# A chunked attention and MLP kernel whose order of issue is planned: fetches of TensorE's instructions enter the plan, two inversions change engine, the filler changes type

## The chip, the cores and the metric

One core of a Trainium2 chip runs the kernel. The metric is device time in microseconds of one execution, the median of three runs. TensorE is called PE below, VectorE DVE, ScalarE ACT, GpSimd POOL; SP is the engine whose queue issues every DMA of this kernel.

## The reference

```
for t in range(768):                                  # state: [4, 8, 40, 40], from zeros
    y[t]  = einsum('bhd,bhde->bhe', r[t], state)
    Sa    = einsum('bhde,bhe->bhd', state, a[t])
    state = state * w[t] - einsum('bhd,bhe->bhde', Sa, b[t]) + einsum('bhd,bhe->bhde', v[t], k[t])
x  = y as [4, 768, 320]
xn = (x - mean) / sqrt(var + 1e-6) * g_ln             # over the 320
out = x + relu(xn @ w_ch1) @ w_ch2                    # w_ch1 320x1280, w_ch2 1280x320
```

All data are fp32: 32 heads (4 x 8) of 40, 768 steps.

## The kernel before

The 768 steps are cut into 24 chunks of 32. Inside a chunk the recurrence is a triangular system for each head. `prep` scales the inputs of a chunk by running products of w (`L436`, `L445` scans on DVE; `aT` at L454 and `bk` at L464 on DVE or POOL) and PE multiplies them (`tri`, L492); DVE puts the result into `gk`, and a DMA writes it to DRAM as `d_g`. The chunks of a **slab** are inverted together: the slabs are chunks 0-1, 2-3, 4-7, 8-11, 12-15, 16-19 and 20-23, numbered 0 to 6 here and in the code. A DMA (L526) brings a slab's matrices into `yi`, one per partition; `invert` runs elimination steps on them, two instructions each; a DMA (L558) writes `d_tt`, and a DMA per chunk (L575) loads the inverse as `tt`.

Slabs in `HALVES` are inverted by halves: 14 steps, and then each chunk needs three products on PE in a row (`solve`, L645: tt, nn, tt) with a copy between them. The other slabs take 30 steps, and their chunks need one product. `BY_POOL` says which slabs run on POOL; the rest run on DVE. Chunk after chunk, `chain` computes prh (L630), the solve, the new state (st, L673) and transposes, and the state feeds the next chunk; `post` (z at L741, y at L764) gives the chunk's output.

Every two chunks make a group for the MLP: `norm`, and `moe` with 80 matmuls at L995 (l1) and 60 at L972 (l2), with high and low parts in fp32r. Group 0 can start when chunks 0 and 1 are through and the weights have been split into such parts (`weights`: ACT, DVE, and PE's `low` at L858 to L881).

What sets the order: `Plan` holds every piece of work as a task with an engine, an assumed length, what it reads and writes, and a due time. `lay` walks through assumed time and lets each engine take the ready task with the earliest due time; for PE it switches between wide tasks (`l1`, `l2`, `low`) and narrow ones by what PE did in the last 3 us (`NEED`, `ENOUGH`). Where PE has nothing between 6 and 165 us of assumed time, it emits a filler matmul (`unit`). The instructions are then issued in the planned order, so each engine's queue, SP's too, is in order on the chip. The plan is made when the kernel is built; nothing is decided on the chip.

```
HALVES = (0, 1, 2)
BY_POOL = (3, 4, 5, 6)
USE = dict(l1=2048, l2=960, ...)        # what a PE task counts towards NEED and ENOUGH
```

Of the kernel before, what the change touches and what calls it, by code (L numbers as in the profile page):

```python
# [23 lines left out]
D = 40  # L24
CH = 320
# [9 lines left out]
HALVES = (0, 1, 2)  # L35
BY_POOL = (3, 4, 5, 6)
# [6 lines left out]
PERIOD, END = 20.5, 500.0  # L43
STRETCH = 1.5
SPAN, NEED, ENOUGH = 3.0, 1900, 4500
TURN, ALIKE = 0.1, 8.0
UNITS = (6.0, 165.0)
BACKLOG = 2.0
SLACK = 0.1
PASSES, MARGIN = 1, 4.0  # L50


class Plan:
# [4 lines left out]
    USE = dict(l1=2048, l2=960, nt=384, tri=320, z=320, st=364, prh=480, solve=160, y=520, kbt=100, pq=340, ss=83, ut=80, low=1000)  # L58
    SHARED = ("g", "q", "aT", "kb", "inv", "rs")
# [66 lines left out]
    def lay(self, soon, unit):  # L126
# [20 lines left out]
        last = None  # L147
        events = [0.0] + [t["t0"] for t in T if t["t0"]]
# [43 lines left out]
        while n_done < n:  # L192
# [3 lines left out]
            while moved:  # L196
                moved = False
                for e in self.ENGINES:
# [5 lines left out]
                    if e == "PE":  # L204
# [27 lines left out]
                    if got is None:  # L232
                        if e == "PE" and unit and UNITS[0] <= now < UNITS[1] and banks:
                            order.append((now, len(order), unit, heapq.nsmallest(1, banks)[0]))
                            free[e] = now + 0.28
# [6 lines left out]
                    if e == "PE":  # L242
# [3 lines left out]
                        last = t["of"]  # L246
                    if e == "POOL" or e == "DVE" and t["of"] in self.SHARED:
# [61 lines left out]
def body(ctx, tc, et_in, vr, rd, vt, w1, w1x_in, w2, gl, fe, fd, out):  # L309
# [92 lines left out]
    def clear(t, keys, eng=("ACT",), t0=18.0):  # L402
# [20 lines left out]
    def prep(c):  # L423
        t, tb = wa[c % 2], bk[c % NBK]
        kw, kbk = [("wa", c % 2, hf) for hf in range(2)], [("bk", c % NBK, hf) for hf in range(2)]
# [69 lines left out]
        task("PE", tri, 0.96, r=kbk + [("aT", c % 2)], bank=(f"pg{c}_0", f"pg{c}_1"), of="tri")  # L495
# [21 lines left out]
    def invert(si):  # L517
# [9 lines left out]
            r=[("d_g", si, k) for k in range(len(SLABS[si]))], w=[ky], of="y_in", land=4.0)  # L527
# [25 lines left out]
        def ones(e, b):  # L553
# [5 lines left out]
            r=[ky], w=[("d_tt", si)], of="tt_out", land=4.0)  # L559
# [155 lines left out]
    def post(c):  # L715
# [29 lines left out]
        task("PE", z, 0.96, r=[(x, hf) for x in ("vuv", "x5r") for hf in range(2)]  # L745
# [41 lines left out]
    def weights():  # L787
# [3 lines left out]
        def gl_(e, b):  # L791
# [3 lines left out]
            nc.scalar.mul(out=minus, in_=ident, mul=-1.0)  # L795
        task("ACT", gl_, 1.45, r=["ident"], w=["gt", "minus"], of="gl")
# [225 lines left out]
    def setup():  # L1022
# [17 lines left out]

        def under(e, b):
# [23 lines left out]
        for t, k in [(wa[i], ("wa", i)) for i in range(2)] + [(bk[i], ("bk", i)) for i in range(NBK)]:  # L1065
            def gap(e, b, t=t):
                (nc.gpsimd if e == "POOL" else nc.vector).memset(t[32:64], 1.0)
            task([("POOL", 0.8), ("DVE", 0.6)] if k[0] == "bk" else "DVE", gap, 0.6, w=[k + (hf,) for hf in range(2)], of="setup",
                 t0=[0.0, 3.0, 9.0, 16.0, 28.0, 36.0, 44.0][k[1]] if k[0] == "bk" else 0.0)
# [193 lines left out]
```

## Time and profile before

| | |
|---|---|
| median of 3 runs | 649.31 us (646.39 to 651.42) |
| the profiled execution | 649.18 us, its span 647.3 us |
| PE busy, share of the span | 578.8 us, 89% |
| DVE, ACT, POOL busy | 381.9, 330.8, 196.3 us |
| TensorE's mean granted clock | 0.910 |
| first l1 matmul, last chunk's y, last l2 matmul end | 143.5, 602.3, 640.9 us |

The profile is of one execution. Its span runs from the first to the last instruction, and 1.9 us of the execution lie outside it. PE is the engine to look at: it is busy nearly all the time, but at a half clock a busy microsecond does half the work, and a wait of PE shows as idle time with the releaser named.

### The profile page before, as it was taken

To read this page: it belongs to the slowest core of one execution; us is meant where nothing else is said; L and a number is where in the kernel's file an instruction comes from. 1 tells how busy PE (TensorE), PEld (TensorE's weight loads), DVE (VectorE), ACT (ScalarE), POOL (GpSimd) and SP (SyncE) were. 2 spreads that over 40 slices of the span, in tenths; PEclk is the share of its full clock that TensorE was granted. 3 is DMA by queue.
4 is the path that set the end of the run, shared out by engine and by line. 5 is a ranking of instruction groups with operands and counts; after the bars stand their busy time and mean duration, and the time that the engine had idled before them with its cause. 6 is when DMAs were issued, how large, how long until landed. Compare 5 with 4: busy or idle time off the path is not lost.

```text
span 647.3 us, 30770 instructions
## 1 busy us (share of the span) xinstructions
PE 578.8 (89%) x13538; PEld 532.8 (82%) x13538; DVE 381.9 (59%) x870; ACT 330.8 (51%) x840; POOL 196.3 (30%) x305
## 2 busy tenths in 40 slices
PE   6989697899979899999698889999799989999995
PEld 6869586688979788889687788989798888999995
DVE  6667476667846555576487465768453644444421
ACT  4765455556544346475386335674456543643320
POOL 4121112211231881231882218822088200000000
PEclk9789676778979888899699788999799999999998
DMA  8989861846577455497765775767643642311000
GB/s 206 275 180 231 207 152 43 201 94 154 124 171 178 100 122 135 109 182 168 158 137 129 165 162 127 165 144 151 144 105 78 147 110 74 61 55 26 23 21 24
DMA packets 127179, 84.82 MB, mean 131 GB/s; under 512 B 94912, under 2 KB 105152, under 8 KB 127040
## 3 DMA queue, kind: packets, MB, share of 16 engines
q1 hardware_dynamic: 127040, 82.80, 55.6%
q8 instruction: 108, 1.77, 1.2%
q14 instruction: 31, 0.25, 0.1%
HBM read 56.67 MB, written 18.24 MB: 116 GB/s over the span
## 4 chain that ended last, share of the span: by engine, by line
PE 64%; issue 4%; DMA 4%; ACT 3%; SPq 3%; DVE 3%; ACTq 0%; DVEq 0%
PE ps L995 17%; PE ps L972 15%; PE ps L673 4%; PE ps L645 4%; PE ps L741 4%; DMA tt<-d_tt 3%; PE ps L600 3%; PE ps L492 3%; PE ps L630 2%; PE ps L724 2%; PE ps L764 2%; PE ps L697 2%; PE ps L1116 1%; PE ps L944 1%; PE ps L476 1%
## 5 line engine op out<-in xcount | busy, mean ns | idle before, releaser
L995 PE MATMUL ps<-xh,w 128*128 128x256 f32 x480 | 116.6, 304 | 2.5 <-issue 2.0
L972 PE MATMUL ps<-w,hh 128*128 128x320 f32 x480 | 116.3, 329 | 0.6 <-ACT hh L1000 0.5
L1004 DVE SCALAR_TENSOR_TENSOR hl<-ps,hh 128x256 fp32r<-128x256 f32 x120 | 50.2, 422 | 93.0 <-ACT hh L1000 92.0
L1000 ACT ACTIVATE hh<-ps 128x256 fp32r<-128x256 f32 x120 | 45.8, 384 | 108.5 <-PE ps L995 105.7
L995 PEld LDWEIGHTS ps<-xh,w 128*128 128x128 f32 x480 | 88.1, 202 | 4.7 <-issue 2.1
L972 PEld LDWEIGHTS ps<-w,hh 128*128 128x128 f32 x480 | 82.0, 197 | 3.1 <-ACT hh L1000 0.7
L972 PE MATMUL ps<-w,hl 128*128 128x320 f32 x240 | 77.1, 321 | 0.0
L546 POOL TENSOR_TENSOR ytmp<-yi 128x30 f32<-128x30 f32 (+14 forms) x120 | 63.0, 525 | 41.0 <-DMA yi<-d_g 32.1
L550 POOL TENSOR_TENSOR yi<-yi,ytmp 128x30 f32<-128x30 f32 (+14 forms) x120 | 68.7, 573 | 9.4
L995 PE MATMUL ps<-xl,w 128*128 128x256 f32 x240 | 70.8, 295 | 0.0
L464 POOL TENSOR_TENSOR bk<-bk,gE 112x1024 f32<-112x1024 f32 x14 | 31.7, 2268 | 113.4 <-DVE gE L436 69.6
L1116 PE MATMUL ps<-start,ident 128*128 128x160 f32 x300 | 58.4, 350 | 5.7 <-POOL ident masks.py:199 3.1
L1116 PEld LDWEIGHTS ps<-start,ident 128*128 128x128 f32 x300 | 50.9, 224 | 8.9 <-POOL ident masks.py:199 3.1
L645 PE MATMUL ps<-hv,tt 32*32 32x40 f32 x2048 | 29.6, 210 | 28.0 <-DMA tt<-d_tt 16.5
L753 DVE TENSOR_TENSOR x5s<-ps,mask 64x256 f32<-64x256 f32 x96 | 40.5, 422 | 22.0 <-PE ps L741 20.4
L683 DVE TENSOR_TENSOR x<-ps,x2s 40x320 f32<-40x320 f32 x92 | 44.8, 487 | 12.4 <-PE ps L673 10.3
L645 PEld LDWEIGHTS ps<-hv,tt 32*32 32x32 f32 x2048 | 24.6, 115 | 32.5 <-issue 16.9
L995 PEld LDWEIGHTS ps<-xl,w 128*128 128x128 f32 x240 | 48.7, 203 | 0.2 <-issue 0.2
L705 ACT COPY xk<-ps 40x320 f32<-40x320 f32 x92 | 38.7, 421 | 19.1 <-PE ps L697 15.9
L972 PEld LDWEIGHTS ps<-w,hl 128*128 128x128 f32 x240 | 47.4, 198 | 0.4 <-DVE hl L1004 0.4
L606 ACT COPY xk<-ps 64x320 f32<-64x320 f32 x96 | 40.4, 421 | 12.3 <-PE ps L600 8.0
L731 ACT COPY vu<-ps 40x256 f32<-40x256 f32 x96 | 35.1, 366 | 18.1 <-PE ps L724 16.5
(132 smaller groups left out, 1102.9 us busy)
## 6 DMA issues: line engine op xcount, KB each, us to landing
wa<-in_et_dram SPq DMA_DIRECT2D x48, 195.2 KB
bk<-in_et_dram SPq DMA_DIRECT2D x48, 192.0 KB
xk<-xk SPq DMA_DIRECT2D x48, 160.0 KB
x<-in_vt_dram SPq DMA_DIRECT2D x48, 128.0 KB
d_g<-gk SPq DMA_DIRECT2D x48, 128.0 KB
d_a<-aT SPq DMA_DIRECT2D x48, 99.0 KB
x2s<-d_a SPq DMA_DIRECT2D x48, 99.0 KB
vu<-in_vr_dram SPq DMA_DIRECT2D x48, 96.0 KB
```

The source lines that it names most:

```text
L546: g.tensor_tensor(out=tv, in0=y[:, j + 1:, j:j + 1].broadcast_to([n, m, j]), in1=y[:, j:j + 1, 0:j].broadcast_to([n, m, j]), op=ALU.mult)
L550: g.tensor_tensor(out=yv, in0=yv, in1=tv, op=ALU.add)
L606: nc.scalar.copy(out=xk1[ro:ro + 64, hf, par::2], in_=banks[b[name]][64 * par:64 * par + 64, 0:CH].rearrange("p (i e) -> p i e", e=D))
L645: nc.tensor.matmul(o[qs, h], lhsT=mat[qs, h], rhs=vec[qs, h], start=True, stop=True)
L683: nc.vector.tensor_tensor(out=x2[n][r0:r0 + D, hf, 8 * pp:8 * pp + 8, 0:D], in0=banks[b[name]][r0:r0 + D, 0:CH].rearrange("p (h e) -> p h ...
L705: nc.scalar.copy(out=xk0[i][r0:r0 + D, hf, par::2], in_=banks[b[name]][rp:rp + D, 0:CH].rearrange("p (k e) -> p k e", e=D))
L753: nc.vector.tensor_tensor(out=x5s[ro:ro + 64, hf, 8 * pp:8 * pp + 8], in0=pz[64 * pp:64 * pp + 64], in1=mask[64 * pp:64 * pp + 64].unsquee ...
L972: nc.tensor.matmul(banks[b[name]][:, 0:CH], lhsT=l[:, us], rhs=ws[f"w2_{f}"][:, y], start=f == 0 and x == 0, stop=f == 9 and x == 2)
L995: nc.tensor.matmul(ph, lhsT=l, rhs=r, start=x == 0, stop=x == 7)
L1000: nc.scalar.activation(out=hhs[n], in_=banks[b[name]][:, 0:256], func=AF.Relu)
L1004: nc.vector.scalar_tensor_tensor(out=hls[n], in0=banks[b[name]][:, 0:256], scalar=0.0, in1=hhs[n].bitcast(F32), op0=ALU.max, op1=ALU.subtract)
L1116: nc.tensor.matmul(banks[b][:, 0:160], lhsT=ident, rhs=flat(start0)[:, 0:160], start=True, stop=True)
```

## The change

`Plan` now counts PE's instructions (`COUNT`) in blocks of 256, of which the first has 63 gone, and assumes that a block cannot begin sooner than `FETCH` = 4.1 us after the one before it. A task that would wait over 0.3 us for this is passed over for one that would not. `PASSES` goes from 1 to 2: the second pass knows when tasks came in the first, and the better of the two plans is taken. `HALVES` and `BY_POOL`: slab 1 is inverted by halves on POOL (DVE before), slab 2 whole on POOL (by halves on DVE before). The filler becomes one fp32r matmul of 320 columns (one fp32 matmul of 160 columns before), assumed at 0.16 us, and may now stand in place of narrow work. Each DMA is assumed to land 1.5 us later. The rows of `wa` and `bk` that no data reach were set by memsets of DVE and POOL; now 18 small DMAs bring ones from the host's padding. Some clearing may move from ACT to POOL, `minus` is made earlier, and five numbers of the plan differ.

```diff
-HALVES = (0, 1, 2)
-BY_POOL = (3, 4, 5, 6)
+HALVES = (0, 1)
+BY_POOL = (1, 2, 3, 4, 5, 6)
-PERIOD, END = 20.5, 500.0
+CLR = 18.0
+EXTRA = 1.5
+PERIOD, END = 21.5, 500.0
-SPAN, NEED, ENOUGH = 3.0, 1900, 4500
-TURN, ALIKE = 0.1, 8.0
+SPAN, NEED, ENOUGH = 3.0, 1600, 4500
+TURN, ALIKE = 0.1, 4.0
+FILL, ULEN = 2600, 0.16
+FETCH, WAIT = 4.1, 0.3
-PASSES, MARGIN = 1, 4.0
+PASSES, MARGIN = 2, 4.0
...
+    COUNT = dict(l1=16, l2=6, nt=6, tri=128, z=128, prh=128, solve=128, st=64, y=128, kbt=16, ss=16, ut=16, pq=8, low=8)
...
+        block = [63, 0.0]
+        def fetched(t, at, do):
+
+            n, us = (self.COUNT[t["of"]], t["where"][0][1]) if t else (2, ULEN)
+            n += t is not None
+            have, began = block
+            wait, pos = 0.0, 0
+            while have + n - pos >= 256:
+                pos += 256 - have
+                x = max(at + wait + us * pos / n, began + FETCH)
+                wait = x - at - us * pos / n
+                began, have = x, 0
+            if do:
+                block[:] = [have + n - pos, began]
+            return wait
...
-                        can = [t for t in can if (t["of"] in self.WIDE) == wide] or can
+                        all_ = can
+                        of = [t for t in can if (t["of"] in self.WIDE) == wide]
+                        fill = wide and not of and use < FILL and UNITS[0] <= now < UNITS[1] and banks
+                        can = [] if fill else of or can
...
+                        if got and fetched(got, now, False) > WAIT:
+                            got = next((t for t in all_ if fetched(t, now, False) < 0.1), got)
...
-        return task("SP", lambda e, b: emit(), 0.4, r, w, of=of, kb=us, land=land, shift=shift, due=due, t0=t0)
+        return task("SP", lambda e, b: emit(), 0.4, r, w, of=of, kb=us, land=land + EXTRA, shift=shift, due=due, t0=t0)
...
-        for t, k in [(wa[i], ("wa", i)) for i in range(2)] + [(bk[i], ("bk", i)) for i in range(NBK)]:
-            def gap(e, b, t=t):
-                (nc.gpsimd if e == "POOL" else nc.vector).memset(t[32:64], 1.0)
...
+            for p in (48, 56):
+                dma(lambda t=t, p=p, cs=cs: sync.dma_start(out=t[p:p + 8], in_=et_in[0, 0, D:48, cs]), 0.1,
+                    w=[k + (p,)], of="gap")
...
-            banks[b][:, 0:160], lhsT=ident, rhs=flat(start0)[:, 0:160], start=True, stop=True)
+            banks[b][:, 0:CH].rearrange("p (k x) -> p k x", x=64), lhsT=minus,
+            rhs=minus[:, 0:64].unsqueeze(1).broadcast_to([128, 5, 64]), start=True, stop=True)
```

Lines shift by the edit: L645 becomes L672, L972 L998, L995 L1021, L546 and L550 L573 and L577. Three places show the new order.

PE's queue in chunk 6 (slab 2) before, around the second and third of its three products.

```order
L972 MATMUL ps_67<-w_7_1628,hh_135 128x320 x2
L972 MATMUL ps_67<-w_7_1628,hl_138 128x320
L645 MATMUL ps_68<-hv_101,nn 32x40 x32
L697 MATMUL ps_69<-ident,x_0_91 104x40 x8
L944 MATMUL ps_70<-ident,xn_128 128x128 x3
L476 MATMUL ps_71<-ident,qc 128x104 x4
L645 MATMUL ps_68<-hv_100,tt_113 32x40 x32
L995 MATMUL ps_72<-xh_130,w_0_4_1674 128x256
```

PE's queue at the same chunk in the changed kernel.

```order
L1021 MATMUL ps_69<-xl_132,w1x 128x256
L791 MATMUL ps_70<-xk_1_98,x5s 32x40 x32
L672 MATMUL ps_68<-hv_100,tt_113 32x40 x32
L724 MATMUL ps_69<-ident,x_0_91 104x40 x8
L503 MATMUL ps_70<-ident,qc 128x104 x4
L998 MATMUL ps_66<-w_6_1751,hh_134 128x320 x2
L998 MATMUL ps_66<-w_6_1751,hl_137 128x320
L998 MATMUL ps_67<-w_6_1751,hh_134 128x320 x2
L998 MATMUL ps_67<-w_6_1751,hl_137 128x320
```

Of three products in a row two are gone with the copies between them; one product remains, after y of the chunk before.

POOL's queue at the end of slab 4 (chunks 12 to 15), before: `yi` and `ytmp` are the elimination, `bk` and `aT` belong to later chunks.

```order
L546 TENSOR_TENSOR ytmp_112<-yi_109 128x58
L550 TENSOR_TENSOR yi_109<-yi_109,ytmp_112 128x2x29
L546 TENSOR_TENSOR ytmp_112<-yi_109 128x30
L550 TENSOR_TENSOR yi_109<-yi_109,ytmp_112 128x30
L556 MEMSET yi_109 128x32
L464 TENSOR_TENSOR bk_89<-bk_89,gE 112x1024
L454 TENSOR_TENSOR aT_106<-wa_83,qE 112x512
```

The same place in the changed kernel.

```order
L577 TENSOR_TENSOR yi_109<-yi_109,ytmp_112 128x5x26
L573 TENSOR_TENSOR ytmp_112<-yi_109 128x108
L577 TENSOR_TENSOR yi_109<-yi_109,ytmp_112 128x4x27
L481 TENSOR_TENSOR aT_106<-wa_83,qE 112x512
L573 TENSOR_TENSOR ytmp_112<-yi_109 128x84
L577 TENSOR_TENSOR yi_109<-yi_109,ytmp_112 128x3x28
L573 TENSOR_TENSOR ytmp_112<-yi_109 128x58
L577 TENSOR_TENSOR yi_109<-yi_109,ytmp_112 128x2x29
L573 TENSOR_TENSOR ytmp_112<-yi_109 128x30
L577 TENSOR_TENSOR yi_109<-yi_109,ytmp_112 128x30
L583 MEMSET yi_109 128x32
```

An `aT` of a later chunk now stands inside slab 4, ahead of its last six instructions. Slabs 3 and 5 had a `bk` ahead of their last two before, and now have an `aT` and a `bk`, and a `bk`, ahead of their last six; slabs 2 and 6 are in one piece.

SP's queue between the write of slab 0's inverse (`d_tt`) and its first load (`tt`), before; `r` are pieces of the weights.

```order
L558 DMA d_tt_182<-yi_109 64x32x32
L420 DMA bk_90<-in_et_dram 48x1024 x2
L812 DMA r_7_768<-in_w_dram 128x320
L806 DMA r_0_4_777<-in_w_dram 128x256
L812 DMA r_6_784<-in_w_dram 128x320
L812 DMA r_8_794<-in_w_dram 128x320
L812 DMA r_9_805<-in_w_dram 128x320
L575 DMA tt_113<-d_tt_182 128x1x256
L526 DMA yi_109<-d_g_176 64x32x32
```

The same place in the changed kernel, up to shortly before that load.

```order
L585 DMA d_tt_182<-yi_109 64x32x32
L536 DMA d_g_176<-gk_108 64x512 x2
L838 DMA r_4_830<-in_w_dram 128x320
L832 DMA r_1_1_845<-in_w_dram 128x256
L832 DMA r_1_2_853<-in_w_dram 128x256
L832 DMA r_0_2_859<-in_w_dram 128x256
L832 DMA r_0_3_869<-in_w_dram 128x256
L832 DMA r_1_3_880<-in_w_dram 128x256
L838 DMA r_5_892<-in_w_dram 128x320
L553 DMA yi_109<-d_g_176 64x32x32
L447 DMA wa_82<-in_et_dram 48x1041 x2
L541 DMA d_a_155<-aT_105 48x528 x2
```

Seven pieces of weights stand there now instead of five, and the load of slab 1 into `yi` has moved ahead of the load of `tt`.

## Rows read from the trace of the kernel before

**Rows 1.** The page: busy times; clock and GB/s by slice; the instruction queue.
```profile
PE 578.8 (89%) x13538; PEld 532.8 (82%) x13538; DVE 381.9 (59%) x870; ACT 330.8 (51%) x840; POOL 196.3 (30%) x305
...
PEclk9789676778979888899699788999799999999998
...
q8 instruction: 108, 1.77, 1.2%
```
**Rows 2.** Stretches: length, busy us (instructions) of each engine, clock, DMA share, GB/s.
```profile
74.00:143.50 69.50, 60.18 (x1427) 51.22 (x1427) 44.63 (x114) 38.67 (x102) 10.94 (x8) 0.74 0.54 129
143.50:602.30 458.80, 420.69 (x11087) 391.20 (x11076) 272.43 (x612) 238.22 (x611) 165.21 (x271) 0.94 0.57 127
602.30:640.90 38.60, 38.09 (x343) 37.08 (x342) 12.91 (x35) 10.12 (x26) 0.24 (x1) 1.00 0.05 18
```
**Rows 3.** PE in order of time, 212 to 222 us: start, length, operation [idle before].
```profile
212.24 0.28 PE L645 MATMUL ps<-hv,tt 32*32 32x40 f32 x8 [2.03 <-issue]
...
217.21 0.79 PE L645 MATMUL ps<-hv,nn 32*32 32x40 f32 x64
217.93 0.80 PE L764 MATMUL ps<-xk,x5s 128*32 128x40 f32 x64
218.66 1.13 PE L492 MATMUL ps<-aT,bk 40*64 40x32 f32 x64
219.73 0.40 PE L645 MATMUL ps<-hv,tt 32*32 32x40 f32 x20
221.34 0.62 PE L645 MATMUL ps<-hv,tt 32*32 32x40 f32 x44 [1.21 <-issue]
```
**Rows 4.** PE's waits, 143.5 to 602.3 us: total us, times, longest.
```profile
PE ps L645 <- DMA tt<-d_tt: 10.8, 4, 4.1
PE ps L645 <- issue: 8.9, 7, 2.0
...
PE ps L673 <- issue: 0.3, 1, 0.3
```
**Rows 5.** The chain at slabs 2 and 6: start, us, what.
```profile
180.26 5.87 DMA tt<-d_tt
...
187.55 3.71 PE ps L995 x16
...
515.57 4.45 DMA tt<-d_tt
```
**Rows 6.** The chain, steps at the full clock.
```profile
348.71 1.06 PE ps L741 x64
...
381.84 0.79 PE ps L645 x64
...
603.12 2.09 PE ps L995 x16
...
635.50 2.64 PE ps L972 x18
```
**Rows 7.** PE in order of time, 44 to 82 us: fillers, the first solve.
```profile
48.79 8.34 PE L1116 MATMUL ps<-start,ident 128*128 128x160 f32 x58
...
73.96 1.29 PE L645 MATMUL ps<-hv,tt 32*32 32x40 f32 x64 [5.72 <-DMA tt<-d_tt]
```
**Rows 8.** Inversion alone (tile yi): stretch, busy us; POOL slabs 4 and 5, DVE slab 2.
```profile
305.20:344.90 39.70, 34.97 (x61) 0.87 0.69 152
386.40:438.20 51.80, 33.77 (x61) 0.96 0.62 144
...
152.00:169.00 17.00, 7.12 (x30) 0.90 0.42 98
```
**Rows 9.** POOL in order of time, inside slabs 3 and 5.
```profile
261.91 2.19 POOL L464 TENSOR_TENSOR bk<-bk,gE 112x1024 f32<-112x1024 f32 x1 [16.70 <-PE ps L697]
...
435.33 2.20 POOL L464 TENSOR_TENSOR bk<-bk,gE 112x1024 f32<-112x1024 f32 x1 [11.27 <-DVE gE L436]
```

More of the change, by code (lines that the diff above doesn't have):

```diff
@@ L234, in lay @@
                             order.append((now, len(order), unit, heapq.nsmallest(1, banks)[0]))
-                            free[e] = now + 0.28
+                            free[e] = now + ULEN + fetched(None, now, True)
                             last = None
@@ L246, in lay @@
                         last = t["of"]
+                        us += fetched(t, now, True)
                     if e == "POOL" or e == "DVE" and t["of"] in self.SHARED:
@@ L399, in dma, with clear @@
     def dma(emit, us, r=(), w=(), of="", land=2.5, shift=0.0, due=None, t0=0.0):
-        return task("SP", lambda e, b: emit(), 0.4, r, w, of=of, kb=us, land=land, shift=shift, due=due, t0=t0)
-    def clear(t, keys, eng=("ACT",), t0=18.0):
+        return task("SP", lambda e, b: emit(), 0.4, r, w, of=of, kb=us, land=land + EXTRA, shift=shift, due=due, t0=t0)
+    def clear(t, keys, eng=("POOL", "ACT"), t0=CLR):
         n = 1
@@ L424, in prep @@
         t, tb = wa[c % 2], bk[c % NBK]
-        kw, kbk = [("wa", c % 2, hf) for hf in range(2)], [("bk", c % NBK, hf) for hf in range(2)]
+        kw, kbk = [("wa", c % 2, hf) for hf in (0, 1, 48, 56)], [("bk", c % NBK, hf) for hf in (0, 1, 48, 56)]
         n = 528
@@ L494, in tri @@
                             lhsT=tb[HR[hf], 64 * p:64 * p + 64], rhs=a[HR[hf], C * p:C * p + C], start=True, stop=True)
-        task("PE", tri, 0.96, r=kbk + [("aT", c % 2)], bank=(f"pg{c}_0", f"pg{c}_1"), of="tri")
+        task("PE", tri, 1.06, r=kbk + [("aT", c % 2)], bank=(f"pg{c}_0", f"pg{c}_1"), of="tri")
         gk = gks[c % 2]
@@ L526, in invert @@
         dma(lambda: sync.dma_start(out=y, in_=d_g[si][1].rearrange("a m t -> m a t")), wire(32 * n, 128),
-            r=[("d_g", si, k) for k in range(len(SLABS[si]))], w=[ky], of="y_in", land=4.0)
+            r=[("d_g", si, k) for k in range(len(SLABS[si]))], w=[ky], of="y_in", land=2.5)
         eng = "POOL" if by_pool else "DVE"
@@ L558, in invert @@
         dma(lambda: sync.dma_start(out=d_tt[si].rearrange("a m t -> m a t"), in_=y), wire(32 * n, 128),
-            r=[ky], w=[("d_tt", si)], of="tt_out", land=4.0)
+            r=[ky], w=[("d_tt", si)], of="tt_out", land=3.0)
     def loads(c):
@@ L744, in z @@
                             start=True, stop=True)
-        task("PE", z, 0.96, r=[(x, hf) for x in ("vuv", "x5r") for hf in range(2)]
+        task("PE", z, 1.06, r=[(x, hf) for x in ("vuv", "x5r") for hf in range(2)]
              + [("vuu", hf, par) for hf in range(2) for par in range(2)], bank=(f"pz{c}_0", f"pz{c}_1"), of="z")
@@ L794, in gl_ @@
                 nc.scalar.mul(out=dgs[k], in_=ident, mul=gt[:, k:k + 1])
-            nc.scalar.mul(out=minus, in_=ident, mul=-1.0)
-        task("ACT", gl_, 1.45, r=["ident"], w=["gt", "minus"], of="gl")
+        task("ACT", gl_, 1.2, r=["ident"], w=["gt"], of="gl")
         def rawx():
@@ L1039, in setup @@
         task("POOL", lambda e, b: make_identity(nc, ident), 1.0, w=["ident"], of="setup")
+        task("ACT", lambda e, b: nc.scalar.mul(out=minus, in_=ident, mul=-1.0), 0.3, r=["ident"], w=["minus"], of="setup")
         def under(e, b):
@@ L1063, in setup @@
                   + [("xk0", i, "s", hf, par) for hf in range(2) for par in range(2)])
-        for t, k in [(wa[i], ("wa", i)) for i in range(2)] + [(bk[i], ("bk", i)) for i in range(NBK)]:
-            def gap(e, b, t=t):
-                (nc.gpsimd if e == "POOL" else nc.vector).memset(t[32:64], 1.0)
-            task([("POOL", 0.8), ("DVE", 0.6)] if k[0] == "bk" else "DVE", gap, 0.6, w=[k + (hf,) for hf in range(2)], of="setup",
-                 t0=[0.0, 3.0, 9.0, 16.0, 28.0, 36.0, 44.0][k[1]] if k[0] == "bk" else 0.0)
+        for t, k, cs in ([(wa[i], ("wa", i), slice(0, 1041)) for i in range(2)]
+                         + [(bk[i], ("bk", i), slice(1041, 2065)) for i in range(NBK)]):
+            for p in (48, 56):
+                dma(lambda t=t, p=p, cs=cs: sync.dma_start(out=t[p:p + 8], in_=et_in[0, 0, D:48, cs]), 0.1,
+                    w=[k + (p,)], of="gap")
         def eye(e, b):
```

## The prediction

> **What bounds the kernel now.** I read the page first [rows 1]: PE is busy for 89% of the span and the chain that ends last runs mostly through it, so the span is PE's work plus what PE loses. The table of stretches [rows 2] cuts the span where the work changes: 74.0 us until the first solve, 69.5 us until the first l1 matmul, 458.8 us in which recurrence and MLP are interleaved, 38.6 us in which the MLP alone runs at a clock of 1.00, and 6.4 us of output.
>
> In the interleaved stretch PE is idle for 458.8 - 420.7 = 38.1 us. The view of PE's waits [rows 4] says why: 10.8 us in four waits for a `tt`, and waits named "issue", 8.9 us of them at L645 and less at five other lines, 16.5 us together. The rest are short joints of the recurrence. PE in order of time shows what an "issue" wait is [rows 3]: nothing that the profile shows holds the solve at 212.24, which begins after 2.03 us idle, and nothing the one at 221.34. Between the two lie 255 matmuls and as many weight loads. Over the run such waits always begin at the same place modulo 256 in PE's instructions, and PE's 27,076 records come to 251 for each of the 108 packets of the instruction queue [rows 1]. So PE's instructions arrive in blocks of 256, and dense runs of small matmuls use them up faster than they come; two blocks in these 9.1 us is at least 4 us for each. An fp32 matmul of the recurrence is two records of each kind, so the 64 of one L645 step alone are 128 instructions.
>
> The third loss is the clock. It is granted at 0.94 in this stretch and 0.74 in the one before [rows 2]. [...]
>
> **The change part by part.** The sum is made against the profiled execution's span of 647.3 us, and 1.9 us lie outside it; its 649.18 us stand 0.13 below the median.
>
> *PE's work.* From the first l1 on, eight solves disappear (chunks 4 to 7, two each): 8 x 0.79 us [rows 6] = 6.3 us, and 1,024 of 27,072 instructions. Fillers there change by less than a microsecond, so I take **-6**. The filler itself: 300 records of 8.34/58 = 0.144 us each [rows 7] become 304 whole matmuls of twice the columns. For those no row stands; by columns and by the row for two records, 0.14 to 0.29 us each, so 44 to 88 us against 43. The low end is nearest to a type that takes 256 columns in 2.09/16 = 0.13 us [rows 6], thus 0.16. All stand before the last 480 us, in stretches with room, so I take 0, and up to +8 for those ahead of the first solve.
>
> *Until the first solve.* It waits 5.72 us for `tt` [rows 7] in a stretch that moves 220 GB/s [rows 1]. In SP's queue before that load stand 0.6 MB more than before, as the changed order shows (weights come in another order and the load of slab 1 is ahead), which is 2.8 us; the loads of `wa` no longer wait for a DVE memset, worth 1 to 2 us. I take **+1**, from -3 to +6.
>
> *From there to the first l1.* PE is idle for 9.3 us of 69.5 and loses about 18 us to the clock [rows 2]; the planned PE work is 40 us in both orders, so the limit is when slab 1's inverse and the split weights arrive. Slab 1 leaves DVE for POOL; DVE, busy for 44.6 us of these 69.5 (POOL 10.9) [rows 2], gets room for splitting weights. By halves on DVE slab 2's instructions take 7.1 us within 17 elapsed [rows 8]; on POOL no half appears, and I estimate 9 to 10 us from the share of a whole slab's 34 us that 14 narrower steps make up. Two more pieces of weights wait behind others. I take **-4**, from -15 (the whole loss goes but a part) to +9.
>
> *Fetching.* Summing over the blocks what each has less than 4.1 us of work, I get 41.2 us for the order before and 31.6 for the changed one. PE hides most of this behind earlier blocks: 16.5 us were measured of 41.2. In the same ratio 12.7 us remain: **-4**, from 0 to -10. The plan counts one instruction more for each task than is issued (750 tasks, against some 165 waits that are instructions), so its blocks drift by two over the run against the chip's; this is why I take no more.
>
> *Waits for `tt`.* Before, 10.8 us in four waits [rows 4], up to 5.87 each on the chain [rows 5]. What a slab has to do between its last `tri` and its first solve is filled by PE with 41.0, 71.8, 70.5, 69.9 and 56.0 us of work for slabs 2 to 6 before, and 64.3, 66.1, 70.0, 67.5 and 58.5 after (order rows by their durations). Slab 2 has 23 us more, for an inversion that takes 39.7 to 51.8 us on POOL [rows 8] and not 17: equal to what it needs within some microseconds. Slabs 3 and 5 have 6 and 2 less and slab 6 2.5 more. The plan now lets transfers land 1.5 us later, which brings loads forward where there is room. I take **-4** of the 10.8, from -10.8 to +8.
>
> [...]
>
> *The end* is 38.6 us of MLP at the full clock, with the same matmuls behind the last y: 0.
>
> Sum: 647.3 + 1 - 4 - 6 - 4 - 4 - 5 = 625.3, and 1.9 outside the span gives **627 us**.
>
> **The rivals.**
> *The gain is given back.* The time from a slab's last `tri` to its `tt` is made of POOL's instructions and four transfers; PE doing less in it waits longer. For it: the wait for `tt` ends last at slabs 2, 4, 5 and 6 already, and slab 6's 4.45 us [rows 5]. Then work, fetch and clock give some 15 us and the waits take back 8 to 10: 638 to 643, say 640. Against it: the change moves y and MLP work into these places.
>
> *Slower: POOL waits inside a slab.* Before, slabs 3 and 5 each had one `bk` among their steps, and POOL's queue, which is in order, stood there for 16.70 and 11.27 us until its data came [rows 9]. Now slab 3 has an `aT` and a `bk`, slab 4 an `aT` (which had none), slab 5 a `bk`, ahead of six instructions of the inversion. Each waits for what PE or DVE produce for a later chunk. If POOL stands there for 11 us more than the slack in each of the three, and PE's work around it runs at the half clock after, that is 3 x 11 us on 625, 658 us. It decides from 8 us for each slab, where the gain of 22 is used up. Against it: in slab 5 the wait was there before, and the wait for `tt` was no longer than at slab 4.
>
> [...]
>
> [...]
>
> *The plan does not do what it says.* With the drift of two blocks the fetch term is nil, and the changed numbers only shuffle tasks: 627 + 4 + 2 = 633 if the rest holds, and 647 to 650 if the first two terms go the other way as well.
>
> **How the numbers follow.** One per cent, 6.5 us, is about what a measurement of this kernel can tell from no change. The forecast, 616 to 637, has 0.46; better than that, where slab 1's earlier inverse and the clock give all they can, 0.10; the gain given back or slab 2 late, 637 to 643, 0.18; no change, 643 to 656, 0.14; slower, 0.12. Faster is thus 0.74, same 0.14, slower 0.12. The range leaves out half of the better and most of the slower cases: 606 to 650; the forecast's own is 616 to 637.
>
> **What would show it.** PE's waits named "issue" would come to some 13 us after the first l1; the waits for `tt` to about 7; the first l1 matmul would start near 140 and the first solve near 75; PE's busy time would fall by some 10 us or more. In POOL's order, idle time ahead of `aT` and `bk` inside slabs 3 to 5 over 10 us would speak for the slower rival, and a wait for `tt` over 10 us at chunk 4 for slab 2 being late. The prediction is wrong if the stretch from first solve to first l1 grows, or if the half-clock share stays where it is though the waits shrink.

## The result and the profile after

The changed kernel takes 633.58 us in the median of 4 runs (621.85 to 640.92), the kernel before 650.37 us beside it: a ratio of 0.962 (0.950 to 0.975). Run again with the first experiments it took 628.72 us, ratio 0.965 (0.959 to 0.971). A ratio compares only the faster executions of both kernels, those within 1.5% of each one's fastest, so it can differ from the ratio of the medians. The profiled execution of the first set took 638.31 us, with a span of 636.6 us at a mean granted clock of 0.906; I therefore read the execution recorded with the first experiment too, called the second execution below (span 628.5 us at 0.922). Lines shift with the edit: L645 is L672 now, L972 L998, L995 L1021.

The page of the changed kernel, with the lines that answer to [rows 1].

```profile
PE 582.8 (92%) x13030; PEld 534.1 (84%) x13030; DVE 363.4 (57%) x795; ACT 324.0 (51%) x828; POOL 241.2 (38%) x398
...
PEclk9869975978996889779999999898987999999998
...
q8 instruction: 104, 1.70, 1.2%
```

PE has 1,016 fewer records on its two rows together and four blocks of instructions fewer, but it isn't less busy: 582.8 us for 578.8, at a mean granted clock of 0.906 for 0.910.

The stretches that answer to [rows 2]: first solve to first l1, from there to the last y, and the MLP alone. First of the profiled execution of the changed kernel, then of the one recorded again.

```profile
79.80:141.50 61.70, 58.79 (x1481) 49.59 (x1482) 38.87 (x82) 37.38 (x100) 31.89 (x53) 0.72 0.71 167
141.50:590.60 449.10, 422.83 (x10509) 392.50 (x10508) 256.98 (x567) 230.03 (x590) 186.94 (x313) 0.92 0.58 126
590.60:629.90 39.30, 37.34 (x300) 36.45 (x287) 12.54 (x35) 9.78 (x25) 0.24 (x1) 1.00 0.04 14
```

```profile
79.10:137.20 58.10, 55.16 (x1482) 47.10 (x1483) 38.27 (x81) 37.43 (x100) 33.01 (x55) 0.78 0.76 176
137.20:582.30 445.10, 415.82 (x10509) 386.02 (x10508) 258.33 (x567) 230.32 (x589) 184.84 (x311) 0.94 0.59 127
582.30:621.60 39.30, 37.35 (x295) 36.44 (x282) 12.48 (x35) 9.79 (x25) 0.24 (x1) 1.00 0.04 14
```

Against [rows 2] the second execution gives: first solve 5.1 us later (79.1 for 74.0), the stretch to the first l1 11.4 us shorter (58.1 for 69.5), the interleaved stretch 13.7 us shorter (445.1 for 458.8), and 1.2 us more after it. That is -18.8, the whole difference of the spans (628.5 for 647.3). The clock of the interleaved stretch is the same 0.94.

PE's waits in the interleaved stretch of the second execution, for [rows 4].

```profile
PE ps L672 <- issue: 6.2, 4, 2.9
PE ps L672 <- DMA tt<-d_tt: 6.2, 2, 5.0
PE ps L657 <- issue: 3.4, 2, 2.8
PE ps L519 <- issue: 2.7, 2, 1.6
```

With five smaller rows the issue waits are 19.0 us (17.8 in the first execution), against 16.5 before: they did not shrink. The waits for `tt` went from 10.8 to 6.2 us. PE idles for 29.3 us in this stretch, 38.1 before; so waits that are neither fell from 10.8 to 4.1, and the busy time by 4.9 us.

### The profile page after: what moved, and what is told of

The parts are those of the page before. It is cut to its first block, busy times and chain, and to the rows that moved or that the text cites. A ratio compares the mean times of both kernels' runs of the same rounds, so it can differ in the third digit from the quotient of the medians.

```text
span 636.6 us, 29775 instructions
## 1 busy us (share of the span) xinstructions
PE 582.8 (92%) x13030; PEld 534.1 (84%) x13030; DVE 363.4 (57%) x795; ACT 324.0 (51%) x828; POOL 241.2 (38%) x398
## 4 chain that ended last, share of the span: by engine, by line
PE 79%; DMA 7%; issue 4%; SPq 3%; ACT 3%; DVE 3%; ACTq 0%; DVEq 0%
PE ps L1021 19%; PE ps L998 18%; PE ps L700 5%; PE ps L768 4%; PE ps L672 4%; PE ps L627 4%; PE ps L519 3%; PE ps L1144 3%; PE ps L751 3%; PE ps L791 3%; PE ps L724 3%; PE ps L657 3%; PE ps L906 2%; DMA tt<-d_tt 2%; PE ps L503 2%
## 5 line engine op out<-in xcount | busy, mean ns | idle before, releaser
L1021 PE MATMUL ps<-xh,w 128*128 128x256 f32 x480 | 117.9, 307 | 4.2 <-DVE x5s L780 2.8
L998 PE MATMUL ps<-w,hh 128*128 128x320 f32 x480 | 117.5, 332 | 2.0 <-DVE hl L1030 1.5
L573 POOL TENSOR_TENSOR ytmp<-yi 128x30 f32<-128x30 f32 (+9 forms) x150 | 77.4, 516 | 50.1 <-DMA yi<-d_g 39.0
L1021 PEld LDWEIGHTS ps<-xh,w 128*128 128x128 f32 x480 | 88.6, 203 | 7.4 <-DVE x5s L780 3.1
L577 POOL TENSOR_TENSOR yi<-yi,ytmp 128x58 f32<-128x58 f32 (+9 forms) x164 | 89.1, 543 | 12.9
L998 PEld LDWEIGHTS ps<-w,hh 128*128 128x128 f32 x480 | 82.8, 199 | 4.8 <-DVE hl L1030 1.9
L998 PE MATMUL ps<-w,hl 128*128 128x320 f32 x240 | 77.3, 322 | 0.0
L1021 PE MATMUL ps<-xl,w 128*128 128x256 f32 x240 | 71.1, 296 | 0.1
L1144 PE MATMUL ps<-minus 128*128 128x320 f32 x304 | 61.6, 349 | 4.7 <-ACT minus L1067 4.4
L481 POOL TENSOR_TENSOR aT<-wa,qE 112x512 f32<-112x512 f32 x20 | 25.3, 1264 | 102.6 <-DVE qE L472 41.8
L1144 PEld LDWEIGHTS ps<-minus 128*128 128x128 f32 x304 | 51.5, 212 | 8.3 <-ACT minus L1067 4.4
L491 POOL TENSOR_TENSOR bk<-bk,gE 112x1024 f32<-112x1024 f32 x15 | 33.0, 2200 | 66.0 <-DVE gE L463 28.1
L780 DVE TENSOR_TENSOR x5s<-ps,mask 64x256 f32<-64x256 f32 x96 | 40.5, 422 | 18.5 <-PE ps L768 16.8
L1021 PEld LDWEIGHTS ps<-xl,w 128*128 128x128 f32 x240 | 49.0, 204 | 0.3 <-DVE xl L978 0.3
L633 ACT COPY xk<-ps 64x320 f32<-64x320 f32 x96 | 40.3, 420 | 16.6 <-PE ps L627 10.8
L998 PEld LDWEIGHTS ps<-w,hl 128*128 128x128 f32 x240 | 47.9, 200 | 0.2 <-DVE hl L1030 0.2
L672 PE MATMUL ps<-hv,tt 32*32 32x40 f32 x1792 | 24.9, 207 | 18.4 <-DMA tt<-d_tt 9.7
```

Source lines behind the costliest of these rows:

```text
L573: g.tensor_tensor(out=tv, in0=y[:, j + 1:, j:j + 1].broadcast_to([n, m, j]), in1=y[:, j:j + 1, 0:j].broadcast_to([n, m, j]), op=ALU.mult)
L577: g.tensor_tensor(out=yv, in0=yv, in1=tv, op=ALU.add)
L633: nc.scalar.copy(out=xk1[ro:ro + 64, hf, par::2], in_=banks[b[name]][64 * par:64 * par + 64, 0:CH].rearrange("p (i e) -> p i e", e=D))
L672: nc.tensor.matmul(o[qs, h], lhsT=mat[qs, h], rhs=vec[qs, h], start=True, stop=True)
L780: nc.vector.tensor_tensor(out=x5s[ro:ro + 64, hf, 8 * pp:8 * pp + 8], in0=pz[64 * pp:64 * pp + 64], in1=mask[64 * pp:64 * pp + 64].unsquee ...
L998: nc.tensor.matmul(banks[b[name]][:, 0:CH], lhsT=l[:, us], rhs=ws[f"w2_{f}"][:, y], start=f == 0 and x == 0, stop=f == 9 and x == 2)
```

## The experiments

Each was timed in five rounds against the kernel before on the same chip, whose median was 652.5 to 655.9 us there; ratios are to this kernel. The experiments ran on three chips, so differences between them are taken from the ratios, at 651 us for the kernel before; such a difference is known to some 6 us.

**The changed kernel again.** No edit.

> The changed kernel once more, for the spread of its time and a second trace. Its first four times run from 621.9 to 640.9 us, and span times granted clock was 577 to 585 us in each, so if the spread is the clock alone, the product stays within 575 to 587 here too while the span moves by up to 20 us; if waits come and go between executions, the product moves with the span.

628.72 us, ratio 0.965 (0.959 to 0.971). Span times granted clock was 579 to 584 us in the six executions while the span moved from 624.0 to 631.9. With the first four, it was 577 to 585 us over spans from 620.1 us (at 0.936) to 639.2 us (at 0.911): the spread goes with the clock. What moves the clock from one execution to the next is not shown.

**Without the count of blocks.** The plan is made anew with this number, so the whole order differs; this holds for every experiment whose edit is one of the plan.

```diff
-FETCH, WAIT = 4.1, 0.3
+FETCH, WAIT = 0.0, 0.3
```

> The changed kernel with FETCH = 0, so that the plan no longer counts blocks of instructions; all else as changed. Theory (counting blocks pays): the shortfall of the blocks against 4.1 us goes from 31.6 to 38.5 us in the order, so waits named issue grow by 3 to 4 us and the time with them, to about 4 us over the changed kernel. Rival (the plan's blocks drift from the chip's, and what is gained is chance): within 2 us of the changed kernel, on either side.

640.05 us, ratio 0.981 (0.974 to 0.987): some 10 us over the changed kernel, more than the theory had. Issue waits in the interleaved stretch were 26.3 us, 7.3 more. Two of its rows, and that stretch:

```profile
PE ps L519 <- issue: 6.1, 6, 2.4
...
PE ps L768 <- issue: 4.7, 3, 2.4
```

```profile
146.50:591.50 445.00, 410.35 (x10284) 381.51 (x10278) 257.75 (x567) 224.73 (x576) 180.01 (x303) 0.95 0.58 127
```

The waits stand at `tri` (L519) and z (L768), steps of 64 records of small fp32 matmuls; in the changed kernel `tri` waits for 2.7 us and z not at all. But they don't show as a longer stretch: it takes 445.0 us, and 445.1 in the changed kernel, with 225 fewer matmul records in it and a clock of 0.95 for 0.94. The whole difference of the two spans (637.7 for 628.5) stands ahead of the first l1, at 146.5 for 137.2. So the plan that counts is some 10 us faster; that it is so through these waits is not shown.

**The old slabs in the changed kernel.**

```diff
-HALVES = (0, 1)
-BY_POOL = (1, 2, 3, 4, 5, 6)
+HALVES = (0, 1, 2)
+BY_POOL = (3, 4, 5, 6)
```

> The changed kernel with slabs 1 and 2 as before (both by halves on DVE), all else as changed. Theory (the slabs carry the gain): 8 solves more on PE are 6.3 us, with their fetching some 9, and the time goes back to 642 to 648. Rival (order of issue, filler and pass carry it): within 4 us of the changed kernel, so 630 to 638.

639.73 us, ratio 0.979 (0.973 to 0.984): some 9 us over the changed kernel. That lies between the two expectations, and nearer to the rival's 638 than to the theory's 642.

**The new slabs alone.** The edit above, the other way, in the kernel before.

> The kernel before with slab 1 by halves on POOL and slab 2 whole on POOL, nothing else changed. Theory (the slabs carry the gain): 636 to 642, 8 to 13 us below the kernel before, eight solves being 6.3 us of it. Rival (the gain of the solves is given back in waits for tt unless the plan's other numbers make room): 646 to 652, with waits for tt over 15 us where the kernel before has 10.8.

649.96 us, ratio 0.990 (0.985 to 0.995): some 6 us below the kernel before. That lies between the two expectations, and the noise does not tell it from the 9 us that the same slabs are worth in the changed kernel.

```profile
PE ps L645 <- DMA tt<-d_tt: 12.2, 3, 6.7
PE ps L645 <- issue: 8.7, 6, 2.9
```

```profile
138.00:596.90 458.90, 419.86 (x10493) 388.90 (x10496) 261.37 (x575) 232.94 (x597) 170.34 (x299) 0.93 0.57 125
```

The interleaved stretch is as long as before (458.9 for 458.8 us), and the 5.5 us by which the span is shorter (641.8 for 647.3) stand ahead of the first l1. So what the solves save there is given back, but not in the way the rival had it: the waits for `tt` are 12.2 us where they were 10.8, not over 15, while with the smaller rows issue went from 16.5 to 22.0 and the clock from 0.94 to 0.93.

**Neither the slabs nor the count.** Both edits in the changed kernel (`FETCH = 0.0`, old slabs).

> The changed kernel with FETCH = 0 and slabs 1 and 2 as before; what is left of the change is the filler, the ones by DMA, the second pass and the plan's numbers. The order falls short of 4.1 us by 45.0 us, against 41.2 in the kernel before. Theory (slabs and counting make the whole gain, each about 0.015): ratio 0.99 to 1.00. Rival (the rest carries part of the gain, as the slabs alone gave 0.990 and not 0.985): 0.975 to 0.985.

659.64 us, ratio 1.000 (0.992 to 1.008), with issue waits of 26.5 us. What is left of the change (filler, ones by DMA, second pass, numbers) gives nothing that can be measured. The four corners are 1.000, 0.981 (slabs), 0.979 (count) and 0.965 (both): the two parts add up, nearly. Each corner is a plan of its own, and how far the time of two plans differs by the chance of their order was not measured, so a part of each difference may be that.

**The count mended.** The plan counts one instruction for each task that PE doesn't execute.

```diff
-            n += t is not None
+            n += 0.23 * (t is not None)
```

> The changed kernel, whose plan now counts 0.23 instruction for each task beside its matmuls and loads, not 1 (some 170 of 750 tasks put a wait of their own into PE's queue). The order's blocks fall short of 4.1 us by 21.6 us, against 31.6. Theory (fetching sets these waits, and the plan loses by counting wrong): waits named issue fall from 21 us to about 15, and the ratio from 0.965 to 0.95 to 0.96. Rival (the gain that the first four experiments show for counting is chance of the order): within 0.01 of 0.965 on either side, with issue waits unchanged.

625.45 us, ratio 0.964 (0.954 to 0.973), with issue waits of 18.5 us. The theory fell: the order's shortfall against 4.1 us went down by a third and the waits did not follow. The trace of the second execution of the changed kernel has a reason. For each block I took the time from the instruction that begins the block before it to the start of the next packet of the instruction queue, and from there to the block's first instruction. For blocks that PE waited for, the second part was 2.2 us at least, 2.8 in the median. The first was 1.25 us in the median of all blocks and up to 3.4 us for those waited for; of 23 us of such waits over the whole run, some 15 stood behind packets that started over 1.5 us late. Where PE waited, 3.4 to 5.9 us passed from one block's beginning to the next, not 4.1. The delay goes in part with the bytes that the other DMA queues move in the first 3 us of a block (correlation 0.44 over 95 blocks); what else delays it stays open.

**A longer fetch.** The mended count, and:

```diff
-FETCH, WAIT = 4.1, 0.3
+FETCH, WAIT = 5.0, 0.1
```

> The mended count with FETCH = 5.0 and WAIT = 0.1. In the traces a block is ready 2.2 to 3.5 us after its packets start, and these start 0.7 to 3.3 us after the block before it begins, so that the spacing is 3.6 to 6 us and not 4.1; 60% of the wait named issue stands behind fetches that started over 1.5 us late. The order's shortfall against 4.1 us is 16.9 us. Theory (the plan counts rightly but with too short a time): issue waits after the first l1 fall from 19 to 10 to 14, ratio 0.945 to 0.96. Rival (late fetches come where they come, whatever the order): issue waits stay at 17 to 20, ratio 0.96 to 0.97.

620.14 us, ratio 0.954 (0.948 to 0.959), some 7 us below the changed kernel; the interval overlaps that of the mended count alone. All its issue waits in the interleaved stretch with the two longest others, then the stretches from the first solve to the first l1 and on to the last y:

```profile
PE ps L519 <- POOL bk L491: 2.9, 1, 2.9
PE ps L519 <- DVE bk L491: 2.1, 1, 2.1
PE ps L998 <- issue: 1.9, 1, 1.9
...
PE ps L672 <- issue: 1.2, 1, 1.2
...
PE ps L1021 <- issue: 0.2, 1, 0.2
```

```profile
77.90:146.10 68.20, 59.94 (x1620) 50.66 (x1621) 50.10 (x99) 40.41 (x109) 40.18 (x67) 0.76 0.73 171
146.10:574.50 428.40, 407.15 (x10393) 376.60 (x10397) 259.49 (x574) 228.25 (x579) 173.81 (x296) 0.97 0.60 130
```

3.3 us of 19.0 are left, none of the waits for `tt`, the clock is 0.97 for 0.94, and the stretch is 16.7 us shorter than in the changed kernel (614.55 us, the shortest of six executions, against 630.17); part of that is lost ahead of it, where the first l1 comes 8.9 us later. The time is that of the theory. The issue waits fell further than it had, but PE's idle time only from 29.3 to 21.3 us: waits for results of DVE, ACT and POOL, 3.6 us in the changed kernel, are 17.5 us here.

**The old filler in the same order.** Only what a filler emits is that of before.

```diff
-            banks[b][:, 0:CH].rearrange("p (k x) -> p k x", x=64), lhsT=minus,
-            rhs=minus[:, 0:64].unsqueeze(1).broadcast_to([128, 5, 64]), start=True, stop=True)
+            banks[b][:, 0:160], lhsT=ident, rhs=flat(start0)[:, 0:160], start=True, stop=True)
```

> The order of the changed kernel, in which each of the 304 fillers is the one of before (fp32, 160 columns, four instructions in place of two). Theory (both fillers take about 0.15 us a piece at the full clock for each two instructions, and change the clock alike): the first l1 matmul starts 5 to 15 us later, since each filler costs twice as much, and the ratio is 0.98 to 0.99. Rival (fillers only take time in which PE would wait): within 0.005 of the changed kernel. The blocks of instructions move by 608 instructions at the first l1, so the places of the issue waits move as well.

639.78 us, ratio 0.984 (0.977 to 0.992), some 13 us over the changed kernel: the theory's ratio, and not the rival's. PE in order of time shows the longest row of fillers in each, 43 of them: the changed kernel, then this one, then this one's stretches from the start to the first solve and to the first l1.

```profile
50.17 6.91 PE L1144 MATMUL ps<-minus 128*128 128x320 f32 x43
```

```profile
55.16 11.95 PE L1144 MATMUL ps<-start,ident 128*128 128x160 f32 x86
```

```profile
0.00:88.50 88.50, 86.43 (x994) 81.21 (x994) 54.18 (x111) 46.88 (x114) 22.99 (x37) 1.00 0.88 215
88.50:144.50 56.00, 52.52 (x1532) 45.67 (x1532) 39.52 (x84) 37.46 (x101) 31.26 (x51) 0.97 0.69 153
```

A new filler takes 0.16 us and an old one 0.28. With the old ones the clock is 1.00 and 0.97 up to the first l1, and the first solve still comes 9.4 us later, while the stretch to the first l1 is 2.1 us shorter only, at 0.97 for 0.78. So the clock is not what sets that stretch. The first l1 comes 7.3 us later, as the theory had it; why the stretch behind it is 6.5 us longer as well (451.6 us) is not shown.

**Blocks moved by half.** The first 64 fillers are old ones, 128 instructions more.

```diff
+        seen[0] += 1
+        if seen[0] <= 64:
+            nc.tensor.matmul(
+                banks[b][:, 0:160], lhsT=ident, rhs=flat(start0)[:, 0:160], start=True, stop=True)
+            return
```

> The order of the changed kernel, in which the first 64 fillers are those of before, which brings 128 instructions more: from there on each block of 256 ends half a block away from where the plan has it. Theory (the plan gains by laying wide work where a block runs out): issue waits after the first l1 grow from 18 us by 3 to 6, and the time by as much; the order's blocks fall short by 32.3 us against 31.6, which says that it may be less. Rival (the plan's blocks are off by up to two blocks of drift already): no difference in issue waits, time within 3 us.

630.39 us, ratio 0.972 (0.963 to 0.980), with issue waits of 18.1 us. The rival holds for the waits; the times are too near to tell. As the order falls short by nearly the same after the move (32.3 for 31.6 us), this says only that the waits do not hang on exactly where the blocks end.

**No fillers in the same order.**

```diff
             if t is unit:
-                unit(b)
+                continue
```

> The order of the changed kernel without its 304 fillers; nothing of the output hangs on them. With the old filler in their place the clock until the first l1 was near 1.00 and that stretch from chunk 0's y to the first l1 was no shorter (34 us in both). Theory (that stretch is set by the chain of the recurrence and its transfers, not by PE's clock): without fillers the clock there falls under 0.75, the first l1 stays within 3 us of 137, the time within 4 us of the changed kernel. Rival (the fillers hold the clock up for the recurrence): the first l1 5 to 10 us later and the time 5 to 15 us over.

614.49 us, ratio 0.939 (0.931 to 0.947): some 17 us below the changed kernel, and the fastest of all. Neither theory had this. From the start to the first solve, to the first l1 and to the last y:

```profile
0.00:78.00 78.00, 32.09 (x528) 23.42 (x528) 54.85 (x113) 46.45 (x114) 22.89 (x34) 0.90 0.92 221
78.00:131.10 53.10, 43.66 (x1431) 36.05 (x1431) 37.23 (x79) 36.60 (x98) 28.96 (x48) 0.79 0.82 190
131.10:565.90 434.80, 414.02 (x10490) 385.00 (x10488) 257.99 (x569) 231.06 (x591) 190.40 (x316) 0.93 0.60 130
```

The clock between first solve and first l1 is 0.79 without fillers and 0.78 with them: they don't hold it up. Without them the first l1 comes 6.1 us earlier. After it the order is the same but for a few fillers, and the stretch is 10.3 us shorter; its issue waits are 8.6 us for 19.0. Since 608 instructions are gone, the blocks end elsewhere. Moving them by 128, or by 608 the other way with the old filler, left issue waits of 18.1 us. Whether this part is a lucky place of the blocks or a merit of leaving fillers out is not shown; a run with the blocks moved back and no fillers would tell.

**The first load of tt earlier.** In SP's queue, the loads of `tt` for chunks 0 and 1 ahead of the load of `yi` for slab 1.

```diff
+    early = [x for x in by_time if x[2] is not unit and x[2]["of"] == "tt"][:2]
+    at = [x for x in by_time if x[2] is not unit and x[2]["of"] == "y_in"][1]
+    by_time = [x for x in by_time if x not in early]
+    k = by_time.index(at)
+    by_time[k:k] = early
```

> The changed kernel with the loads of tt for chunks 0 and 1 moved in SP's queue ahead of slab 1's load of yi (three to five rows up); nothing else moves. Theory (the first solve is later than before because its load stands behind loads of wa and writes of d_a and d_g that SP's queue, in order, has to issue first): the load is issued near 66 us in place of 74.4, the first solve starts near 74 in place of 79, and the end comes 2 to 5 us earlier. Rival (the transfers are late because the DMA engines are full): the first solve within 2 us of 79. A third: the first solve moves but the end doesn't, since the next chunks wait for slab 1.

629.08 us, ratio 0.967 (0.961 to 0.974). SP's queue in the changed kernel, then here:

```profile
65.62 0.63 SPq L553 DMA_DIRECT2D yi<-d_g  x1
66.36 5.90 SPq L447 DMA_DIRECT2D wa<-in_et_dram  x2
72.35 0.83 SPq L541 DMA_DIRECT2D d_a<-aT  x2
73.28 1.11 SPq L536 DMA_DIRECT2D d_g<-gk  x2
74.44 0.60 SPq L602 DMA_DIRECT2D tt<-d_tt  x1
```

```profile
65.12 1.21 SPq L602 DMA_DIRECT2D tt<-d_tt  x2
66.38 0.62 SPq L553 DMA_DIRECT2D yi<-d_g  x1
```

The load goes out 9.3 us earlier and the first solve starts at 75.3 for 79.1, but the first l1 at 136.0 for 137.2, and the time is the same within the noise. The third expectation holds: these 4 us are hidden by what follows.

**Both: a longer fetch, no filler planned.** The mended count, FETCH and WAIT as above, and no time in which fillers are laid.

```diff
-UNITS = (6.0, 165.0)
+UNITS = (200.0, 200.0)
```

> The mended count with FETCH = 5.0 and WAIT = 0.1, and a plan that lays no filler at all. Leaving the fillers out of the changed order took 14 us and halved the issue waits after the first l1 (18.4 to 9.2 us); the longer fetch took 9 us and left 4.8 us of issue waits. Theory (the fillers cost by themselves: they stand before work that comes ready, and fill blocks): both gains add in good part, 604 to 611 us, ratio 0.925 to 0.935, with issue waits of 3 to 8 us. Rival (without the fillers the blocks only ended elsewhere, and that gain is the same as that of the longer fetch): 613 to 620, ratio 0.94 to 0.95.

631.02 us, ratio 0.966 (0.960 to 0.972): worse than either, and neither expectation. Its first two stretches from the first solve on, in an execution of 640.05 us, the longest of six:

```profile
79.60:145.40 65.80, 57.11 (x1569) 46.59 (x1569) 48.16 (x96) 41.34 (x109) 34.93 (x64) 0.66 0.77 174
145.40:597.20 451.80, 426.68 (x10384) 394.84 (x10383) 259.49 (x572) 228.39 (x582) 172.02 (x297) 0.92 0.57 123
```

Planned without fillers the order is another one: the first l1 comes 14.3 us later than where fillers were only left out, and the issue waits are 13.1 us, not 3.3. A plan in which PE's time runs on without fillers issues other work. Which of its moves costs that was not tried.

## Why the prediction came out right, and where its terms did not

The forecast was 627 us; 633.58 and 628.72 were measured. The sign, the size and the range hold, but several terms of the sum were off and their errors cancelled, so that the size is right is in part luck. I compare each with the second execution above, whose span of 628.5 us is nearest to the forecast's 625.3.

**PE's work, -6.** Busy time in the interleaved stretch fell by 4.9 us at the same granted clock, so this is near. Putting the old slabs back cost some 9 us, in a plan made anew; how much of it is the solves, costed at 6.3, that run does not separate.

**First solve, +1.** It is +5.1, inside the range of -3 to +6. I costed the bytes ahead of the load and let the memsets' end pay for part. The 9 us by which the load is issued later than its place ahead of `yi` would allow pass in SP's queue, which takes 5.90 us to issue two loads of `wa` and then issues `d_a` and `d_g`. I named the weights and the load of slab 1 and not these rows between. It cost nothing in the end, as the moved load shows.

**To the first l1, -4.** It is -11.4, inside its bounds too, and the term most undersized. PE's idle time in it fell from 9.3 to 2.9 us and the clock rose from 0.74 to 0.78. That the clock sets it, as I reckoned with my 18 us, is wrong: with it at 0.97 the stretch was 56.0 us. Where only the fillers were left out it was 53.1 us at 0.79, so the fillers themselves are part of it; the rest I did not isolate. Nor is an early first l1 a gain by itself: with the old slabs it came at 132.9 us, and at 126.1 without the count as well, and the stretch behind it was longer (466.0 and 479.3 us). So that slab 1's move to POOL brought the first l1 forward is not shown. Slab 1 by halves on POOL had this row (its instructions on `yi` alone, 74.4 to 88.5 us); my 9 to 10 us of busy time for it were right:

```profile
74.40:88.50 14.10, 2.62 (x6) 1.13 (x6) 1.17 (x3) 2.08 (x5) 9.98 (x28) 0.76 0.85 256
```

**Fetching, -4.** This step failed: the waits are 17.8 and 19.0 us where 16.5 were. The ratio by which I scaled (measured over shortfall, 16.5 of 41.2) supposed that each block takes 4.1 us. Where PE waits they take 3.4 to 5.9, and a smaller shortfall at 4.1 us doesn't bring less waiting (the mended count) while one planned at 5.0 us does (3.3 us). Yet counting is worth some 10 us within the changed kernel: without it, its plan with the new numbers waits for 26.3 us, and for 26.5 with the old slabs too. Against the kernel before, the plan's other numbers took away what counting gave in waits. My reason for taking no more, the drift of the blocks, is not what matters, since with the count mended the waits stayed at 18.5 us.

**Waits for tt, -4.** -4.6, but not as I had it. Slab 2 on POOL took 39.0 us in the second execution:

```profile
120.40:159.40 39.00, 1.05 (x2) 0.60 (x2) 0.42 (x1) 0.51 (x1) 34.38 (x61) 0.78 0.57 125
```

PE still waits for chunk 4's `tt`, for 4.97 us where it was 3.55. I had taken this for a matter of POOL's time against PE's work. The rows show the inversion's last instruction, the issue of its write, that of chunk 4's load and the solve; behind them stands the solve of the kernel before:

```profile
159.29 0.17 POOL L583 MEMSET yi<- 128x32 f32 x1
...
175.51 0.74 SPq L585 DMA_DIRECT2D d_tt<-yi  x1
...
187.68 0.60 SPq L602 DMA_DIRECT2D tt<-d_tt  x1
...
192.25 1.29 PE L672 MATMUL ps<-hv,tt 32*32 32x40 f32 x64 [4.97 <-DMA tt<-d_tt]
```

```profile
186.26 1.29 PE L645 MATMUL ps<-hv,tt 32*32 32x40 f32 x64 [3.55 <-DMA tt<-d_tt]
```

The inversion was done 9 us earlier than on DVE before (168.5 us), and 28 us before its load went out. In between, its write and its load stood in SP's queue behind other transfers, of which one alone waited 5.0 us for a state step of PE (L700). With the longer fetch PE waited for no `tt`. So here the wait was SP's order, and not POOL. Chunk 4's solve starts at 192 us for 186 before, but its later products are gone, and chunk 4's y comes at 202 us for 218. POOL's steps are the longer ones all the same: one step of slab 1, on DVE before and on POOL in the second execution, takes 0.27 and 0.39 us.

```profile
87.42 0.27 DVE L550 TENSOR_TENSOR yi<-yi,ytmp 64x112 f32<-64x112 f32 x1
```

```profile
80.28 0.39 POOL L577 TENSOR_TENSOR yi<-yi,ytmp 64x112 f32<-64x112 f32 x1
```

**Half clock, -5.** No run shows this term: the clock of the interleaved stretch is 0.94 in both. What the second execution shows is one wait with a clock of 0.50 behind it, here in PE's order of time and in the stretches ahead of it, behind it and after that.

```profile
224.61 0.36 PE L672 MATMUL ps<-hv,tt 32*32 32x40 f32 x9 [2.90 <-issue]
```

```profile
215.00:221.70 6.70, 6.54 (x287) 5.93 (x288) 3.01 (x9) 4.19 (x12) 5.96 (x10) 1.00 0.81 158
224.60:230.40 5.80, 5.79 (x37) 5.62 (x37) 2.36 (x8) 3.73 (x9) 5.17 (x9) 0.50 0.24 48
230.40:236.00 5.60, 5.60 (x116) 5.33 (x116) 3.61 (x6) 4.47 (x12) 4.89 (x10) 1.00 0.10 26
```

PE works without a pause from 224.6 on and is granted 0.50 until 230.4. What a microsecond at 0.50 is worth differs by the matmul. On the chain of this execution 12 matmuls of L998 take 3.24 us in that stretch and 1.96 ahead of the wait:

```profile
213.01 1.96 PE ps L998 x12
...
226.69 3.24 PE ps L998 x12
```

In the kernel before, 14 records of fillers took 4.10 us at 0.50, 0.293 each, for 0.144 at 0.99 [rows 7]. The first row has them; the next two are the stretch that they fill and that of [rows 7].

```profile
19.62 4.10 PE L1116 MATMUL ps<-start,ident 128*128 128x160 f32 x14
```

```profile
19.70:23.60 3.90, 3.90 (x15) 3.86 (x16) 2.35 (x5) 1.37 (x3) 0.00 (x0) 0.50 1.05 275
48.80:57.00 8.20, 8.20 (x61) 8.10 (x60) 6.83 (x20) 4.86 (x13) 0.79 (x1) 0.99 0.91 235
```

By the two times of L998 I estimate that some 2.3 of the 5.8 us behind this wait of 2.90 us went to the clock. But fewer waits in all did not bring a higher clock: PE's idle time in the interleaved stretch fell by 8.8 us, as much as the two terms for waits together (4 and 4), and the clock stayed, which I had named as a sign of being wrong. Nor do the other runs bear it out: the clock was 0.95 with 34.7 us idle (without the count), 0.93 with 20.8 (no fillers) and 0.97 with 21.3 (longer fetch). Which waits are followed by the half clock stays open.

**The rest.** In the interleaved stretch, waits that I had not priced fell from 10.8 to 4.1 us. With the earlier first l1, that made up for fetching, the clock and the later first solve.

**The rivals.** The gain given back in waits for `tt` did not come about; with the slabs alone in the kernel before, what was given back went to issue waits (22.0 us for 16.5). Slab 2 was not late: its steps took 39.0 us. The 51.8 us of one slab before [rows 8] are no sign that POOL's steps ran slower in it: they hold 11.27 us in which POOL waited for the inputs of a `bk` [rows 9], and its busy time, 33.8 us, was less than the 35.0 of the slab that took 39.7. The slower one did not come about: POOL does wait inside slab 3, in the second execution as follows, but `tt` of slab 3 was waited for by nobody, for PE had work.

```profile
244.21 1.18 POOL L481 TENSOR_TENSOR aT<-wa,qE 112x512 f32<-112x512 f32 x1 [7.97 <-DMA x2s<-d_a]
245.35 2.18 POOL L491 TENSOR_TENSOR bk<-bk,gE 112x1024 f32<-112x1024 f32 x1
247.49 0.33 POOL L573 TENSOR_TENSOR ytmp<-yi 128x84 f32<-128x84 f32 x1
```

Before, POOL waited for 16.70 us there [rows 9]. That the plan doesn't do what it says is half true: its fetches are too short and its count drifts, and it gains nevertheless.

What made the time, then: the slabs and the count, some 9 and 10 us when either is taken out, each in a plan made anew, and nothing that can be measured of the rest (1.000, 0.992 to 1.008). By which waits the count pays stays open. Two versions came out below both kernels: the longer fetch, 620.14 us, and the changed order without its fillers, 614.49 us.

## What to carry to other kernels

PE, with some 26,000 records, waited for its own instructions here, for 19.0 us from the first l1 to the last y. The sign is a wait without a releaser at a fixed place: counted over PE's matmuls, weight loads and sequencer records, each such wait of over 0.3 us in the profiled executions of both kernels stands 193 or 194 records past a multiple of 256 (15 waits before, 14 after). With 4.1 us planned for a block, where 3.4 to 5.9 passed, these waits stayed; 5.0 us left 3.3 us of them, though other waits grew. Slab 2's inversion, done 9 us earlier, brought its first solve no sooner, since its load went out 28 us after it. Filler work has to be shown to pay by leaving it out with the order held, which was worth some 17 us here, and a change to a planned order is worth judging by switching its parts off one by one: two parts carried all that could be measured here.

## What was unexpected of the hardware

Where PE waited for a block of 256 instructions in the second execution, 3.4 to 5.9 us had passed since the block before had begun, since the block's packet started up to 3.4 us after that, and the block itself 2.2 us later at the least. A wait of 2.90 us was followed by 5.8 us at a granted clock of 0.50 in unbroken work. Fillers did not raise the clock between the first solve and the first l1 (0.78 with, 0.79 without), though the longer ones did (0.97, with 18.7 us of them there for 14.0), and there the time was no better. Span times granted clock stayed within 1.3% over ten executions whose spans differed by 3.1%.
